# Left-over casts moved behind the last w_out transfer, their stagings moved to a batch's last step, batch 2's middle part reordered in the other half of hbuf

**Chip, cores, metric.** One core of one Trainium2 chip. The metric is the device time of one execution in microseconds (us), lower is better. Times are medians of repeated runs. A profile is one execution; its span, from the first to the last instruction, is about 2 us under the timed figure of the same run.

## The reference

Attention with a "softmax plus one" denominator, then an MLP with exact GELU. Shapes: batch 8, 12 heads, 448 positions, 64 columns per head; d_model 768, d_ff 2048; inputs and output are float32.

```python
scores = scale * q @ k.T ; m = max(scores)
e = exp(scores - m)
attn = e / (sum(e) + exp(-m) + 1e-9)
x = (attn @ v), heads joined          # 3584 x 768
out = gelu(x @ w_in) @ w_out
```

## The kernel before

The kernel works in steps. Step s computes scores and exponentials of one pair of heads; a batch has six pairs (NPAIR = 6). TensorE fills the time in which ScalarE makes exponentials with the MLP of the batch before: in the steps r = 0 and 1 of a batch with layer 1, in the later ones with halves of layer 2 ("l2"). For batch 0 all six steps r = 0 to 5 hold layer 2. Scores run two steps ahead, so step b = 0, r = 4 computes the scores of batch 2's first pair.

448 positions are three full blocks of 128 and 64 left-over rows. Left-over rows of k and v are staged in float32 on SyncE's queue and cast to float16 by GpSimd. All other loads from here on are issued by GpSimd, in program order.

```python
stage_pool = ... bufs=2          # two staging buffers in turn
h_pool     = ... bufs=1          # hbuf0, hbuf1: layer 1's results before GELU

def stage_left(src, b, gate=False):
    st = stage_pool.tile([P, NPAIR, D], FP32, name="stage")
    ...                          # four transfers on SyncE's queue
        nc.sync.dma_start(out=dst, in_=view[i, e])

def cast_left(src, b):
    if src is v:
        nc.gpsimd.tensor_copy(out=vl[b % 2], in_=st)         # one cast
        return
    for x in range(2):                                       # two casts
        nc.gpsimd.tensor_copy(out=blocks[...], in_=st[r]...)
```

Batch 2 comes in three parts (pairs 0 to 2, pair 3, pairs 4 and 5), since its loads arrive while batch 0 still works. VectorE reorders each part into hbuf, which is free at that time, and SyncE's queue transposes it from there:

```python
PARTS = (0, 3, 4, NPAIR)
def order_by_pairs(b, w, c0, c1):
    if w == 0:
        spare = h_pool.tile([P, NBURST * S], FP16, name="hbuf1")
    ...
        nc.vector.tensor_copy(out=dst[:, :, :, e, :], in_=src[:, c0:c1, e])

def fetch_part(b, i):            # i = 0 after batch 0's GELU, 1 in r = 4, 2 in r = 5
    for w in range(2):           # q, then k
        order_by_pairs(b, w, c0, c1)
        transpose_on_dma(b, w, c0, c1)
```

Order of the loads before these steps, and what each step fetches:

```python
load_part(0); load_w_out(0, 0..1)        # first half of w_out's columns
stage_left(v, 1); stage_left(k, 2)
load_v(1, 0, 8); load_w_out(1, 0..3)     # second half, in quarters of d_ff
load_part(1); load_v(1, 8, H); load_part(2)
cast_left(v, 1); cast_left(k, 2)

def fetch(b, r):                         # after step r of batch b
    r0 = 0 if b else 2
    if r == r0 and b + 2 < B:
        stage_left(v, b + 2)
        load_v(b + 2)
    if r == r0 + 1 and b + 2 < B:
        cast_left(v, b + 2)
    ...
    elif b and r in (0, 1) and b + 2 < B:
        transpose_on_dma(b + 2, r)       # r = 0: q; r = 1: k and its left-overs
    if r == 3 and b + 3 < B:
        load_pairs(q ..., b + 3); load_pairs(k ..., b + 3)
        stage_left(k, b + 3)
    if r == 4 and b + 3 < B:
        cast_left(k, b + 3)
```

The softmax here doesn't subtract the row's maximum and nothing guards it: scores larger than these inputs give would overflow.

## Time and profile before

| | |
|---|---|
| median before the prediction | 420.46 us (419.53 to 420.59) |
| the run that was profiled | 421.8 us, span 420.0 us |
| waits of TensorE of 1 us or more after the start | 2.00 us at 66.3, 5.34 us at 89.8 |
| stretch at half clock (granted clock 0.50), begun in the second | 88.3 to 95.2 us |

The lines themselves stand in the prediction. In the slices each digit is the busy share of a fortieth of the span in tenths. A line of the timeline gives start, busy time, engine, source line, operation, what it writes and reads, and in brackets the idle time of the engine before it and what ended that.

### The profile page before, as it was taken

To read this page: it belongs to the slowest core of one execution; us is meant where nothing else is said; L and a number is where in the kernel's file an instruction comes from. 1 tells how busy PE (TensorE), PEld (TensorE's weight loads), DVE (VectorE), ACT (ScalarE), POOL (GpSimd) and SP (SyncE) were. 2 spreads that over 40 slices of the span, in tenths; PEclk is the share of its full clock that TensorE was granted. 3 is DMA by queue.
4 is the path that set the end of the run, shared out by engine and by line. 5 is a ranking of instruction groups with operands and counts; after the bars stand their busy time and mean duration, and the time that the engine had idled before them with its cause. 6 is when DMAs were issued, how large, how long until landed. Compare 5 with 4: busy or idle time off the path is not lost.

```text
span 420.0 us, 11017 instructions
## 1 busy us (share of the span) xinstructions
PE 400.3 (95%) x4679; PEld 247.0 (59%) x4679; DVE 202.5 (48%) x485; ACT 299.5 (71%) x450; POOL 101.2 (24%) x140
## 2 busy tenths in 40 slices
PE   8888998949999999999999999999999999999995
PEld 3444864525566565666566565666766665665663
DVE  4886335539057732477057731477057741540021
ACT  5998887937888776898588676898589576734300
POOL 8751213095431091024601073020000000000000
PEclk9999999979999999999999999999999999999999
DMA  9999999999992899229962899129211100110032
GB/s 154 152 197 199 197 181 178 190 138 166 153 139 77 119 169 111 61 70 181 133 69 62 118 156 138 59 68 170 58 39 39 40 22 18 54 44 20 2 81 70
DMA packets 137312, 45.08 MB, mean 107 GB/s; under 512 B 118384, under 2 KB 137264, under 8 KB 137264
## 3 DMA queue, kind: packets, MB, share of 16 engines
q0 software_dynamic: 81200, 21.11, 54.7%
q1 hardware_dynamic: 55280, 22.66, 29.5%
q8 instruction: 36, 0.59, 0.6%
q10 hardware_dynamic: 784, 0.62, 0.5%
q14 instruction: 12, 0.10, 0.1%
HBM read 45.61 MB, written 11.01 MB: 135 GB/s over the span
## 4 chain that ended last, share of the span: by engine, by line
PE 78%; DMA 15%; POOL 3%; issue 1%; SPq 1%; DVE 1%; POOLq 0%
PE bank L260 62%; DMA vn<-in_v_dram 9%; PE st L358 6%; PE bank L407 5%; DMA w_in_sb<-in_moe_w_in_dram 3%; DMA tqk<-klraw 2%; PE st L429 2%; PE st L260 2%; DMA stage<-in_v_dram 1%; PE bank L422 1%; POOL rawq L98 1%; POOL rawk L98 1%; DMA out_dram<-osb 1%; SPq L305 1%; PE st L407 1%
## 5 line engine op out<-in xcount | busy, mean ns | idle before, releaser
L346 ACT ACTIVATE et<-st,expb 128x896 f16<-128x896 f32 x144 | 134.4, 1002 | 27.8 <-PE st L358 27.6
L260 PE MATMUL bank<-xt,w_in_sb 128*64 128x448 f16 x1536 | 152.8, 355 | 0.0
L260 PEld LDWEIGHTS <-w_in_sb 128*64 128x64 f16 x1536 | 94.8, 110 | 53.7 <-issue 4.6
L260 PE MATMUL bank<-w_out_sb,gt_odd 128*64 128x384 f16 x1024 | 88.0, 326 | 0.0
L512 DVE COPY osb<-bank 128x384 f32<-128x384 f32 x56 | 31.2, 557 | 99.7 <-PE bank L260 97.7
L260 PEld LDWEIGHTS <-gt_odd 128*64 128x64 f16 x1024 | 57.9, 110 | 27.5 <-issue 2.1
L260 PE MATMUL bank<-w_out_sb,gt_even 128*64 128x384 f16 x768 | 68.5, 327 | 0.0
L445 DVE TENSOR_TENSOR xt<-bank,rec 128x448 f16<-128x448 f32 x44 | 27.5, 625 | 79.4 <-PE bank L422 66.2
L260 PEld LDWEIGHTS <-gt_even 128*64 128x64 f16 x768 | 43.3, 110 | 22.2 <-issue 3.3
L358 PE MATMUL st<-tqk 64*64 64x448 f16 x576 | 43.2, 369 | 1.5 <-ACT et L346 0.4
L469 ACT ACTIVATE gt_odd<-bank 128x448 f16<-128x448 f32 (+1 forms) x74 | 29.1, 394 | 21.5 <-PE bank L260 20.6
L346 ACT ACTIVATE el<-st,expb 128x448 f16<-128x448 f32 x48 | 30.7, 639 | 14.3 <-PE st L429 13.7
L392 DVE TENSOR_TENSOR ksum<-ksum,el 64x448 f16<-64x448 f16 x96 | 37.9, 395 | 2.1
L474 DVE COPY hbuf<-bank 128x448 f32<-128x448 f32 x54 | 33.5, 620 | 10.6 <-PE bank L260 10.0
L392 DVE TENSOR_TENSOR ksum<-t,et 128x448 f16<-128x448 f16 x96 | 35.1, 400 | 0.9 <-ACT et L346 0.6
L392 DVE TENSOR_TENSOR t<-et 128x448 f16<-128x448 f16 x96 | 33.3, 388 | 1.1 <-ACT et L346 0.6
L407 PE MATMUL bank<-et,vn 128*64 128x448 f16 x264 | 33.5, 361 | 0.2 <-DVE tqk L280 0.2
L469 ACT ACTIVATE gt_even<-bank 128x384 f16<-128x384 f32 x34 | 16.7, 490 | 21.5 <-PE bank L260 21.5
L114 POOL DMA_DIRECT2D rawq<-in_q_dram x40 | 30.5, 772 | 3.2 <-DMA vn<-in_v_dram 2.9
L436 ACT ACTIVATE rec<-st,oneb 128x448 f32<-128x448 f32 x42 | 26.7, 639 | 4.9 <-PE st L429 4.9
L358 PEld LDWEIGHTS <-tqk 64*64 64x64 f16 x576 | 15.6, 107 | 22.8 <-issue 18.0
L439 ACT ACTIVATE rec<-rec 128x448 f32<-128x448 f32 x48 | 27.6, 577 | 1.5
(62 smaller groups left out, 247.7 us busy)
## 6 DMA issues: line engine op xcount, KB each, us to landing
vn<-in_v_dram POOLq DMA_DIRECT2D x6, 576.0 KB, 8.7
rawq<-in_q_dram POOLq DMA_DIRECT2D x40, 84.0 KB, 7.5
rawk<-in_k_dram POOLq DMA_DIRECT2D x33, 96.0 KB, 7.0
w_in_sb<-in_moe_w_in_dram POOLq DMA_DIRECT2D x4, 768.0 KB, 16.0
out_dram<-osb SPq DMA_DIRECT2D x16, 168.0 KB, 2.2
out_dram<-osb SPq DMA_DIRECT2D x16, 144.0 KB, 2.0
out_dram<-osb SPq DMA_DIRECT2D x16, 120.0 KB, 2.0
w_out_sb<-in_moe_w_out_dram POOLq DMA_DIRECT2D x2, 768.0 KB, 28.0
```

The costliest lines, as they stand in the source:

```text
L114: nc.gpsimd.dma_start(out=dst[:, :, j, e, :], in_=view[j, e])
L260: nc.tensor.matmul(out[x], lhs[:, x], rhs, start=start, stop=stop)
L346: nc.scalar.activation(out=out, in_=in_, func=AF.Exp, bias=expb, scale=scale)
L358: nc.tensor.matmul(st[cols, e, 0:S], kt[r, j, cols], qt[r], start=True, stop=True)
L392: nc.vector.tensor_tensor(out=dst, in0=a, in1=x, op=ALU.add)
L407: nc.tensor.matmul(po_t[g][e * D:(e + 1) * D, 0:S], v_t[b][:, 2 * c + e, j, :], et[:, 2 * j + e], start=(first and j == 0), stop=(not firs ...
L436: nc.scalar.activation(out=rec_t[g], in_=den_t.pop(g)[:, 0:S], func=AF.Ln, bias=oneb, scale=1.0)
L439: nc.scalar.activation(out=rec_t[g], in_=rec_t[g], func=AF.Exp, scale=-1.0)
L445: nc.vector.tensor_tensor(out=xt_t[b][:, c, :], in0=po_t.pop(g)[:, 0:S], in1=rec_t.pop(g), op=ALU.mult)
L469: nc.scalar.activation(out=dst[:, 0, :], in_=ph[:, c0:c1], func=AF.Gelu)
L474: nc.vector.tensor_copy(out=h_t[b, i][:, n, :], in_=ph[:, 0:S])
L512: nc.vector.tensor_copy(out=osb, in_=po[:, 0:NHW])
```

## The change

The intent is threefold: batch 1's cast of v ready before TensorE asks for it; SyncE's queue clear ahead of the middle part's transposes; and the last part's reordering free of the middle part's transposes.

```diff
-    def order_by_pairs(b, w, c0, c1):
+    def order_by_pairs(b, w, c0, c1, buf):
...
-            spare = h_pool.tile([P, NBURST * S], FP16, name="hbuf1")
+            spare = h_pool.tile([P, NBURST * S], FP16, name=f"hbuf{buf}")
...
         load_w_out(1, i, 4)
+    cast_left(v, 1)
+    cast_left(k, 2)
     load_part(1)
     load_v(1, 8, H)
     load_part(2)
-    cast_left(v, 1)
-    cast_left(k, 2)
...
-            order_by_pairs(b, w, c0, c1)
+            order_by_pairs(b, w, c0, c1, 1 - i % 2)
...
-        r0 = 0 if b else 2
-        if r == r0 and b + 2 < B:
+        if r == 0 and b and b + 2 < B:
+            cast_left(k, b + 2)
+            if b == 1:
+                cast_left(v, b + 1)
             stage_left(v, b + 2)
+        if r == (0 if b else 2) and b + 2 < B:
             load_v(b + 2)
-        if r == r0 + 1 and b + 2 < B:
+        if r == 1 and b and b + 2 < B:
             cast_left(v, b + 2)
...
+        if r == NPAIR - 1 and b + 3 < B:
             stage_left(k, b + 3)
-        if r == 4 and b + 3 < B:
-            cast_left(k, b + 3)
+            if b == 0:
+                stage_left(v, b + 2)
```

## The prediction

> **What bounds the kernel now.** I read the page first, then the matmul timeline, because the page says that TensorE is busy 400.3 of 420.0 us. What is left to win is the idle 20 us and any time at a reduced clock. The page's slices show where that is: the first slices, and one stretch near 84 to 100 us where PE drops to 4 tenths and the granted clock to 7.
>
> ```profile
> PE 400.3 (95%) x4679; PEld 247.0 (59%) x4679; DVE 202.5 (48%) x485; ACT 299.5 (71%) x450; POOL 101.2 (24%) x140
> PE   8888998949999999999999999999999999999995
> PEclk9999999979999999999999999999999999999999
> DMA  9999999999992899229962899129211100110032
> ```
>
> The DMA row is full until some 126 us, so data that is wanted early is a possible bound of its own. From 100 us to the end the timeline shows no idle time of PE. Only two waits of 2 us and more lie before that, both in batch 0's layer-2 steps (steps r = 0 to 5, about 54 to 84 us), and both at the product with the left-over rows of v (L422):
>
> ```profile
> 66.30 0.38 PE L422 MATMUL bank<-el,vl 64*64 64x448 f16 x4 [2.00 <-POOL vl L149]
> 89.84 0.58 PE L422 MATMUL bank<-el,vl 64*64 64x448 f16 x2 [5.34 <-DVE osb L512]
> ```
>
> The first waits for GpSimd's cast of batch 1's left-over v. The GpSimd timeline tells why that cast is late: in program order it stands behind the loads of batch 2's parts, and these are held up until older transfers have landed.
>
> ```profile
> 46.53 0.74 POOL L180 DMA_DIRECT2D w_out_sb<-in_moe_w_out_dram  x1 [1.78 <-DMA rawq<-in_q_dram]
> ...
> 64.99 0.74 POOL L98 DMA_DIRECT2D rawk<-in_k_dram  x1 [3.35 <-DMA w_out_sb<-in_moe_w_out_dram]
> 65.73 0.52 POOL L149 CAST vl<-stage 128x384 f16<-128x384 f32 x1
> 66.18 1.07 POOL L154 CAST klraw<-stage 64x384 f16<-64x384 f32 x2
> 67.39 1.02 POOL L98 DMA_DIRECT2D vn<-in_v_dram  x1
> 83.63 0.50 POOL L149 CAST vl<-stage 128x384 f16<-128x384 f32 x1 [15.22 <-DMA stage<-in_k_dram]
> ```
>
> The second is put down to VectorE's copy of an output half (L512), which frees the PSUM bank. VectorE itself stood still: its copies of batch 2's last part into hbuf (L298) waited until the transposes of the middle part had read the same buffer. SyncE's queue issued those late:
>
> ```profile
> 87.41 0.73 DVE L298 COPY hbuf<-rawq 112x512 f16<-112x512 f16 x2 [5.72 <-DMA tqk<-hbuf]
> 88.06 0.41 DVE L298 COPY hbuf<-rawk 128x384 f16<-128x384 f16 x2
> 88.39 0.80 DVE L392 TENSOR_TENSOR ksum<-ksum,el 64x448 f16<-64x448 f16 x2
> 89.22 0.56 DVE L512 COPY osb<-bank 128x384 f32<-128x384 f32 x1
> ```
>
> ```profile
> 72.22 5.79 SPq L143 DMA_DIRECT2D stage<-in_v_dram  x4
> 78.11 1.01 SPq L488 DMA_DIRECT2D out_dram<-osb  x2
> 79.16 3.01 SPq L143 DMA_DIRECT2D stage<-in_k_dram  x4
> 82.40 2.51 SPq L305 DMA_TRANSPOSE tqk<-hbuf  x2
> ```
>
> The middle part was copied by 77.98 us, but its transposes were issued at 82.40: eight staging transfers stood ahead of them in one in-order queue, and some of those waited for earlier landings (the chain of waits has DMA tqk<-klraw, then SPq L143, then DMA stage<-in_v_dram, then SPq L305). So the chain is: casts late, batch 2's left-over transpose late (67.28), stagings late, middle transposes late, VectorE held, bank held, PE idle.
>
> Last, the busy time and clock by stretch:
>
> ```profile
> 84.50:89.80 5.30, 0.00 (x0) 0.00 (x0) 2.31 (x7) 0.88 (x1) 5.30 (x8) 0.86 1.69 124
> 89.80:95.20 5.40, 5.36 (x34) 2.39 (x35) 2.34 (x5) 1.90 (x2) 5.40 (x7) 0.50 2.18 153
> 74.35:83.26 8.91, 8.91 (x118) 5.35 (x113) 6.09 (x20) 8.75 (x14) 0.00 (x0) 1.00 1.07 196
> ```
>
> Columns: stretch, length, busy time of PE, PEld, DVE, ACT, POOL, then PE clock, DMA share, GB/s. The long wait is followed by 5.4 us at half clock.
>
> **What the Trainium skill says.** "TensorE: Matmul & The Clock Gate", section "Part 1: The HAM clock gate", has the clock at half after an idle window of about 3.4 us and full again after about 3.4 us of sustained work. The trace agrees in kind: 0.50 after 5.34 us idle, nothing after 2.00 us; the half-rate stretch lasted 5.4 us here. "DMA: Bandwidth & Descriptors", section "SWDGE vs HWDGE vs iDMA", says that transfers of GpSimd and of SyncE sit in different queues of the same 16 engines, served in turn, so moving one kind earlier makes the other slower. The trace agrees: the four stagings at 34.8 us took a median of 9.1 us to land, those late in the run some 2 us. "GPSIMD Engine Reference", section "4.1 Engine selection", calls one-input elementwise work there roughly line-rate; here 384 columns take 0.52 us, so the casts cost little; only their place matters.
>
> **The change, part by part.** It adds and removes no work: the same casts, stagings and copies, at other places.
>
> 1. *Casts behind the last w_out issue.* That issue ends at 46.53 + 0.74 = 47.27. The staged v and k were issued at 31.95 to 36.72 and land after medians of 7.7 and 9.1 us, so by about 46. The three casts (0.52 + 1.07 = 1.6 us) run at 47.3 to 48.9 and end 17 us ahead of their use. They push the rawq load from 48.06 to 48.9; the next load waits for a landing at 51.9 anyway, so nothing follows. The 2.00 us wait goes. By stretches: 63.26:74.35 takes 11.09 us, the next two steps of the same work 8.91, so **2.2 us**.
> 2. *Middle part in the other half.* Its readers until then, the GELUs of batch 0 from hbuf, end at 50.0 us. The last part's copies then need only the first part's transposes, which landed by 54.46 + 15.8 = 70.3. The 5.72 us wait of VectorE goes.
> 3. *Staging of v2 and k3 in the last step, their casts at r = 0 of the next batch.* SyncE's queue before the middle transposes keeps only output stores, so they go out at about 75.5 (the copies at 77.31, less the 2 us won) instead of 82.40. GpSimd is not held 15.22 us by the cast and issues batch 3's 14 loads from about 73 on instead of 84.
>
> What parts 2 and 3 are worth together: 83.3:113.4 takes 30.1 us; the same passage one batch later (136.4:163.5) takes 27.1 and contains 64 layer-2 matmuls (5.2 us) that batch 1 lacks, so 21.9 without a wait. **8.2 us** = 5.34 idle + 5.4 × (1 − 0.50) = 2.7 of slow clock + 0.2. Sum of both: 10.4 us, all on PE's path: 420.46 − 10.4 = 410.1.
>
> **Rivals: what could take it back.**
>
> - *hbuf0 becomes the wait.* Batch 1's first layer-1 result goes into hbuf0, which the middle transposes now read. I put its need at 84.7 (94.7, less 2.2, 5.3 and half of the 4.9 us at half clock before it); issued at 75.5 and 76.6 with 4 to 9 us to land, they are done by 81 to 86. PE has a second bank, 1.2 us of grace. Against it: at most a few tenths; if the landing takes 13 us, as the first part's did, 2 to 3 us.
> - *Batch 3's transposes become the wait.* Before, they are issued at 96.55, 102.12 and 110.63 and land after 13.6, 14.7 and 9.1 us: k at 116.8, left-overs at 119.7. PE reads them at 125.57 and 128.34, a slack of 8.8 and 8.6 us, less than the 10.4 that PE would gain. If they land at the same times, the gain stops at 8.6 (411.9). And their chain has lengthened: middle transposes, stores, staging k3 (about 84 to 87), cast k3 (about 93), staging v3, transpose of q (about 96). In favour: the DMA engines moved only 124 GB/s in 81.5:91 while GpSimd stood in the cast, against 214 just before and 171 after; filling 9.5 us at some 60 GB/s more takes 0.6 MB, about 3 us, out of the later queue, so I expect k by about 114 against a need of 115.2. Loss 0 to 2 us; I take 0.4.
> - *ScalarE becomes the bound* in 57 to 84 us: busy 8.75 of 8.91 us per two steps. Behind the first wait it lay idle 1.56 and 0.64 us, 2.2 in all, just what PE gains; so no loss beyond a tenth or two.
> - *The waits are hidden anyway or another stands right behind*, say the bank held at L422 by a late load of the last part (k lands at 64.99 + 15.2 = 80.2; VectorE comes to it at about 80). This would leave a short idle, but only over 3 us of it brings the half clock back; 0.2.
>
> **Range and chances.** 410.1 + 0.4 + 0.2 = **410.7 us**. If batch 3 or hbuf0 bind fully the time is 412 to 414; everything clean with a little more won is 409.2. Range 409.2 to 414. Two per cent is 412.05, only 1.3 us above my number, so: faster 0.70, same 0.29, slower 0.01.
>
> **What would show each step.** Casts at about 47 to 49 us with no wait of PE on vl; middle transposes at about 75 to 77 us; no wait of the hbuf copies on tqk<-hbuf; the granted clock at 1.00 throughout 80 to 100 us; batch 3's loads from about 73 us. The prediction is wrong if PE waits anew at about 85 (hbuf L474 behind tqk<-hbuf), or at about 115 to 118 us (scores of batch 3 behind tqk<-rawk or tqk<-klraw), or if a wait over 3 us brings a second stretch at half clock.

## The result

The four runs of the changed kernel took 414.11, 414.33, 421.84 and 424.69 us: median 418.08, against 420.02 of the kernel before in four runs. The ratio of the fast runs, the two of 414 us, is 0.9861, 95% interval 0.9834 to 0.9889; with all four runs the means are 418.74 and 420.04 us, ratio 0.997. If the long runs are the kernel's own, as e1 below supports, the ratio of the fast runs flatters the change. Ratios here are the mean time of one kernel's fast runs over that of the other's of the same rounds, so not quite the ratio of the quoted medians; a run counts as slow when it is over 1.5% above the fastest of its kernel. The profiled run took 414.33 us, span 412.1.

The page of the changed kernel, in the slices of before:

```profile
PE 397.5 (96%) x4679; PEld 248.7 (60%) x4679; DVE 200.8 (49%) x485; ACT 299.4 (73%) x450; POOL 102.3 (25%) x140
PE   7788999999989999999999999999999999999995
PEclk9999999999999999999999999999999999999999
DMA  9999999999997899229991699229611010110032
```

The hole near 84 us and its dip of the clock are gone, and the DMA row is as full as before. GpSimd's timeline and SyncE's queue show the parts of the change where the prediction put them:

```profile
45.99 0.74 POOL L180 DMA_DIRECT2D w_out_sb<-in_moe_w_out_dram  x1 [2.16 <-DMA rawq<-in_q_dram]
46.73 0.52 POOL L149 CAST vl<-stage 128x384 f16<-128x384 f32 x1
47.18 1.08 POOL L154 CAST klraw<-stage 64x384 f16<-64x384 f32 x2
...
73.80 3.85 POOL L114 DMA_DIRECT2D rawq<-in_q_dram  x5 [7.37 <-PE bank L422]
```

```profile
75.78 2.54 SPq L305 DMA_TRANSPOSE tqk<-hbuf  x2
...
99.70 3.38 SPq L305 DMA_TRANSPOSE tqk<-rawq  x1
103.31 7.75 SPq L305 DMA_TRANSPOSE tqk<-rawk  x1
```

Casts at 46.7, middle transposes at 75.8, batch 3's loads from 73.8. But TensorE's timeline has three new waits:

```profile
92.98 11.54 PE L260 MATMUL bank<-xt,w_in_sb 128*64 128x448 f16 x120 [0.92 <-DVE hbuf L474]
...
117.24 0.38 PE L358 MATMUL st<-tqk 64*64 64x448 f16 x4 [0.65 <-DMA tqk<-rawk]
...
120.78 0.38 PE L260 MATMUL st<-tqk 128*64 128x448 f16 x2 [0.60 <-DMA tqk<-klraw]
```

The first is layer 1 of batch 1 held by VectorE, which waits to overwrite hbuf1 until the last part's transposes have read it (10.7 us from issue to landing). The other two are batch 3's scores behind its transposes. In spans: 420.0 less the 10.4 of the two old waits, plus 0.92 + 0.65 + 0.60 and 0.3 of later start, is 412.1, what the trace has. The trace is thus accounted for, within 0.1 us; what it leaves open is why the timed gain of the fast runs is only 5.8 us, and what the runs of 421.8 and 424.7 us are. For the experiments, theory A says that both come from transfers whose landing times vary from run to run and which TensorE now catches up with; theory B, that something outside the kernel makes the long runs.

### The profile page after: what moved, and what is told of

Read it like the earlier page. It is cut to its first block, busy times and chain, and to the rows that moved or that the text cites. A ratio compares the mean times of both kernels' runs of the same rounds, so it can differ in the third digit from the quotient of the medians.

```text
span 412.1 us, 11014 instructions
## 1 busy us (share of the span) xinstructions
PE 397.5 (96%) x4679; PEld 248.7 (60%) x4679; DVE 200.8 (49%) x485; ACT 299.4 (73%) x450; POOL 102.3 (25%) x140
## 4 chain that ended last, share of the span: by engine, by line
PE 82%; ACT 7%; DMA 6%; SPq 2%; DVE 2%; issue 1%; DVEq 0%
PE bank L260 66%; PE st L358 6%; PE bank L407 5%; ACT et L346 4%; DMA tqk<-hbuf 3%; DMA tqk<-klraw 2%; SPq L305 2%; PE st L429 2%; PE st L260 2%; DMA hbuf<-in_k_dram 1%; PE bank L422 1%; ACT el L346 1%; ACT rec L439 1%; PE st L407 1%; DVE ksum L392 1%
## 5 line engine op out<-in xcount | busy, mean ns | idle before, releaser
L260 PEld LDWEIGHTS <-w_in_sb 128*64 128x64 f16 x1536 | 96.9, 110 | 51.6 <-issue 4.4
L358 PE MATMUL st<-tqk 64*64 64x448 f16 x576 | 42.3, 363 | 2.3 <-DMA tqk<-rawk 0.6
L392 DVE TENSOR_TENSOR ksum<-t,et 128x448 f16<-128x448 f16 x96 | 34.1, 391 | 0.9 <-ACT et L346 0.6
L154 POOL CAST klraw<-stage 64x384 f16<-64x384 f32 x12 | 7.3, 611 | 90.2 <-DMA stage<-in_k_dram 88.7
L114 POOL DMA_DIRECT2D rawk<-in_k_dram x30 | 24.6, 823 | 20.2 <-DMA rawq<-in_q_dram 18.9
```

The lines of the kernel that those rows point to most:

```text
L114: nc.gpsimd.dma_start(out=dst[:, :, j, e, :], in_=view[j, e])
L260: nc.tensor.matmul(out[x], lhs[:, x], rhs, start=start, stop=stop)
L358: nc.tensor.matmul(st[cols, e, 0:S], kt[r, j, cols], qt[r], start=True, stop=True)
L392: nc.vector.tensor_tensor(out=dst, in0=a, in1=x, op=ALU.add)
```

## The experiments

Each set shared a chip and the runs of the kernel before. The sets e1 to e4, e5 to e8, e9 to e12 and e13 to e16 had medians of before of 422.45, 421.19, 421.79 and 421.73 us.

| run | what it is | runs, us | ratio to before (95%) |
|---|---|---|---|
| e1 | the change again | 415.01 to 421.55 | 0.9868 (0.9825 to 0.9911) |
| e2 | before again | 419.21 to 423.01 | 0.9962 (0.9918 to 1.0006) |
| e3 | change, transposes first | 411.44 to 417.72 | 0.9779 (0.9734 to 0.9825) |
| e4 | change, own buffers | 412.46 to 424.54 | 0.9785 (0.9730 to 0.9840) |
| e5 | casts alone | 420.80 to 423.65 | 1.0022 (0.9984 to 1.0060) |
| e6 | other half alone | 415.78 to 419.78 | 0.9899 (0.9857 to 0.9941) |
| e7 | casts and half | 415.52 to 416.87 | 0.9871 (0.9844 to 0.9898) |
| e8 | change, both mendings | 411.03 to 415.34 | 0.9809 (0.9770 to 0.9847) |
| e9 | change, casts in other order | 413.71 to 417.70 | 0.9843 (0.9806 to 0.9881) |
| e10 | casts and own buffers | 414.48 to 419.28 | 0.9875 (0.9833 to 0.9917) |
| e11 | e8, no wait on w_out (wrong result) | 410.71 to 412.37 | 0.9749 (0.9719 to 0.9779) |
| e12 | change without the half | 418.76 to 423.23 | 0.9946 (0.9900 to 0.9992) |
| e13 | change, batch 4's loads held | 411.56 to 418.34 | 0.9795 (0.9750 to 0.9841) |
| e14 | e3, batch 4's loads early | 412.88 to 415.25 | 0.9832 (0.9784 to 0.9880) |
| e15 | change, no wait on w_out (wrong result) | 414.16 to 420.19 | 0.9869 (0.9821 to 0.9918) |
| e16 | e8, v of batch 1 split | 411.05 to 413.10 | 0.9768 (0.9735 to 0.9802) |

All but e11 and e15 gave a correct result.

### e1: the change again

No edit.

> The changed kernel unaltered, to see how often it falls into the longer time (421.8 and 424.7 us against 414.1 and 414.3). Theory A: the longer times are the kernel's own: one of the new waits (last part's transposes behind hbuf at about 92 us, batch 3's transposes at about 117 us) grows past 3 us when the transfers are a little slower, and brings a stretch at half clock; then the clock of those runs is 0.985 to 0.990 and a fresh trace shows the same waits with other lengths. Theory B: something outside the kernel; then the kernel before, run beside it, shows such runs as often. Expected: most runs 413.5 to 415.5, some 420 to 425.

Six runs took 418.91, 418.50, 415.01, 416.85, 421.55 and 415.17 us, so three of six are over 418. The eleven runs of before beside them lie between 420.25 and 425.06. Theory B was to be told by before showing as many long runs; it spreads as much, but it has waits of its own, so its spread alone decides nothing. The fresh trace does better. It is of the first of the six, 418.91 us:

```profile
74.10 0.84 PE L260 MATMUL bank<-w_out_sb,gt_even 128*64 128x384 f16 x8 [2.63 <-DMA w_out_sb<-in_moe_w_out_dram]
...
121.28 0.59 PE L358 MATMUL st<-tqk 64*64 64x448 f16 x4 [2.90 <-DMA tqk<-rawk]
```

The busy time by stretch, behind the second of these (columns as in the prediction; the third figure from the end is the granted clock):

```profile
121.30:124.50 3.20, 3.20 (x26) 1.42 (x28) 0.76 (x2) 2.58 (x3) 2.46 (x3) 0.50 1.82 208
```

A wait that the first trace does not have stands at 74.1: the last quarter of w_out's second half. It landed at 74.1 here; in the first trace a median of 24.2 us after its issue at 45.99, so at 70.2, just before TensorE's use at about 71.8 (the second 16 matmuls of that half begin at 71.14 and come to the last quarter midway). And the wait for batch 3's k grew from 0.65 to 2.90 us, with 3.4 us at half clock behind it. Waits and clock are 2.63 + 0.38 (hbuf) + 2.90 + 1.7 = 7.6 us, against 2.2 in the first trace: 5.4 more, and the time is 4.6 more. This supports theory A: the same kernel, the same order, other landing times.

### e2: the kernel before again

No edit.

> The kernel before unaltered, for a second trace. The first trace is of a run of 421.8 us, while its timed runs took 419.5 to 420.6. If my sum was too large because that trace was of a longer run, the second wait of this trace (5.34 us, with 5.4 us at half clock) is shorter here, by 1 to 2 us in all with the slow clock, and the time is about 420. If it is as long as in the first trace, the missing 2 us lie elsewhere.

The profiled run took 419.21 us. Its waits and the stretch behind the first:

```profile
66.43 0.38 PE L422 MATMUL bank<-el,vl 64*64 64x448 f16 x4 [1.98 <-POOL vl L149]
89.56 0.38 PE L422 MATMUL bank<-el,vl 64*64 64x448 f16 x2 [3.25 <-DVE osb L512]
```

```profile
67.50:70.90 3.40, 3.40 (x26) 1.83 (x22) 2.60 (x7) 1.46 (x2) 1.02 (x1) 0.50 1.47 188
```

The second wait is 2.1 us shorter than in the first trace, and the stretch at half clock is 3.4 us, this time behind the short wait. The sum is 1.98 + 3.25 + 3.4 × 0.5 = 6.9 us, where the same terms of the first trace give 2.00 + 5.34 + 2.7 = 10.0 (10.4 when taken by stretches). So the trace that the prediction rested on shows a longer run than most of the timed ones: 421.8 us against a median of 420.

### e3: transposes ahead of the staging

On the changed kernel:

```diff
         if r == 0 and b and b + 2 < B:
             cast_left(k, b + 2)
             ...
-            stage_left(v, b + 2)
         ...
-        if r == 1 and b and b + 2 < B:
-            cast_left(v, b + 2)
         ...
             transpose_on_dma(b + 2, r)
+            if r == 1:
+                stage_left(v, b + 2)
+        if r == 2 and b and b + 2 < B:
+            cast_left(v, b + 2)
```

> The changed kernel, with the next batch's transposes issued ahead of the staging of left-over v (staging after the transposes of r = 1, its cast at r = 2). If the waits at about 117 and 121 us come from the place of batch 3's transposes in SyncE's queue (behind a staging that waits for a cast), they go: transposes at about 95.5, 100.5 and 106 us in place of 99.7, 103.3 and 111.1, and 1.4 + 0.6 = about 1.5 to 2 us are won: 412.0 to 412.8. Rival: the DMA engines are full there anyway and the transposes land no earlier; then 414.

The ratio is 0.9779. The profiled run, 411.44 us, has no wait of TensorE over 0.3 us between 60 and 126 us. The transposes of q, k and left-overs were issued at 93.7, 98.1 and 101.3 us, and that of k landed 10.1 us after issue, at 108. The waits went, as theory A asks. That this came of the place in SyncE's queue is not shown, since the cast of v at r = 2 also put off the loads of batch 4 behind it, from 102 to 111 us; e13 and e14 come back to this. Two of the six runs still took 417.7; they count as slow, so the ratio is of the other four.

### e4: own buffers for the middle and last parts

On the changed kernel:

```diff
-            spare = h_pool.tile([P, NBURST * S], FP16, name=f"hbuf{buf}")
             n = 2 * (c1 - c0)
+            spare = (h_pool.tile([P, NBURST * S], FP16, name=f"hbuf{buf}") if c0 == 0
+                     else h_pool.tile([P, n * (NJ + NK) * D], FP16, name=f"part{buf}"))
```

> The changed kernel, with a buffer of its own for each of batch 2's middle and last parts, so that layer 1's results wait for no transpose. Theory: the wait of 0.92 us at about 92 us (hbuf behind tqk<-hbuf) goes. If the later waits on batch 3's transposes are set by the transfers' absolute times, they grow by as much, and the time stays at 414 (within 0.3); if they are set by the pace of TensorE, 0.9 us are won: 413.2.

The trace, of a run of 413.40 us, has no wait on hbuf, but its wait for batch 3's k is 1.37 us where the first trace of the change had 0.65: most of the 0.92 came back one station later. Three runs took 412.46 to 414.29, the other three 421.15 to 424.54; the ratio rests on the three fast ones and says little. The mending of this wait alone doesn't touch the long runs.

### e5, e6, e7, e12: the parts of the change by themselves

The three parts are the casts (C), the other half (H) and the move of the stagings (S). Their edits are those pieces of the diff above: e5 is C, e6 is H, e7 is C and H, e12 is C and S.

> The kernel before, with the two casts moved alone. My reading: the 2.0 us wait on the cast of v goes (2.2 us), but the middle part's transposes stay behind the eight stagings and come out at about 81 us, so VectorE's copies of the last part still wait for hbuf until about 86, while TensorE comes to the bank at about 82: 4 to 5 us of wait stay. 418 to 420. Rival: the casts are the head of the whole chain, and with them early the second wait goes too: 411 to 413.

The ratio is 1.0022: the casts alone win nothing. The wait on vl is gone from the trace, and the second has grown to 7.06 us, with 10.2 us at half clock:

```profile
88.93 0.58 PE L422 MATMUL bank<-el,vl 64*64 64x448 f16 x2 [7.06 <-DVE osb L512]
```

TensorE comes to the bank 2.6 us earlier (81.9 against 84.5), but is let on only 0.9 us earlier (88.9 against 89.8). The transposes of the middle part were issued at 80.5, as my reading had it, and the rival falls. The time, 420.80 to 423.65, is over the 418 to 420 expected, by the longer wait and its slow clock.

> The kernel before, with the middle part in the other half of hbuf alone. My reading: the second wait (3.3 to 5.3 us and the slow clock behind it) goes, the 2.0 us wait on the cast stays, and batch 3's transposes keep their early place with some 8 us to spare, so nothing new appears: 6 to 8 us less than before, 413 to 415 with before at 421. Rival: the new buffer alone does nothing while the stagings stand ahead of the transposes: 420.

The ratio is 0.9899, 4.3 us: most of what the whole change brings, of one name in one line. But less than the 6 to 8 us expected, and with two waits that I had not put there:

```profile
87.11 2.46 PE L260 MATMUL bank<-xt,w_in_sb 128*64 128x448 f16 x24 [1.11 <-DVE hbuf L474]
96.04 11.54 PE L260 MATMUL bank<-xt,w_in_sb 128*64 128x448 f16 x120 [3.01 <-DVE hbuf L474]
```

With the middle transposes still behind the stagings (81.2 us), both halves are read later than layer 1 wants to write them. In this trace the 2.0 us wait on the cast of v was absent, since the w_out transfer that held GpSimd's queue had landed earlier (61.3 us against 64.7); so that wait too comes and goes with the transfers.

> The change without the move of the stagings and of their casts. If the move of the stagings is what made batch 3's transposes late (issued at 99.7 us in the changed kernel against 96.5 before), they come at about 95 here, no wait at 117 to 121 us appears, and the time is 1 to 2 us under the changed kernel's (about 412 to 413), less up to 1.5 us for hbuf behind the last part's transposes at 91 us. If the move is what frees TensorE at 84 us, the long wait comes back and the time is over 418.

The ratio is 0.9871, the same as the whole change's 0.9868 and 0.9861. As expected, there is no wait for batch 3 in the trace, but 1.55 and 0.78 us on hbuf and 0.92 on w_out. The time expected, 412 to 413 or up to 1.5 us more by hbuf, was missed: the six runs took 415.52 to 416.87. The move of the stagings thus exchanged the wait on hbuf for that on batch 3's transposes and won nothing that these runs show. The comparison has one flaw. In the traces of e7, e9 and e16 the first product of layer 2 comes at 56.5 to 56.8 us, in the other fifteen at 54.8 to 55.8; in e7 TensorE waited 1.69 us for a load of k and ran at half clock from 28.2 to 31.7 us. The program up to there is that of the change, so the start varies from run to run too, by about 1 us here.

> The changed kernel, with the middle part in hbuf1 again: casts and stagings moved, one buffer. The last part's copies then wait for the middle part's transposes, which here land at about 85 us in place of 87, while TensorE comes to the bank at 82: some 4 to 5 us of wait with half clock behind it, 418 to 422. If it is near the changed kernel's 414 to 418, the other half is not needed once the stagings are moved.

The ratio is 0.9946, as expected: the trace has 4.77 us of wait at the bank, behind one of 2.64 us on w_out. The other half is needed with the stagings moved as well.

### e8, e10, e11, e15: what is left when the new waits are mended

e8 joins e3 and e4. e10 is e7 with the own buffers of e4.

> The changed kernel with the transposes ahead of the staging of left-over v, and with own buffers for the middle and last parts. If the waits at 92 us and at 117 to 121 us are the whole of what the change lost, none is left but one on the last w_out transfer (about 70 us) in runs where transfers are slow: 409.5 us of span at best, 411 to 415 timed, at or under the kernel with the transposes ahead alone (411.4 to 417.7), and fewer runs over 418 than the changed kernel has.

The ratio is 0.9809 and all six runs lie between 411.03 and 415.34. The trace, of the longest of them, has one wait left:

```profile
74.07 1.16 PE L260 MATMUL bank<-w_out_sb,gt_even 128*64 128x384 f16 x8 [2.59 <-DMA w_out_sb<-in_moe_w_out_dram]
```

> The kernel before, with the casts moved and own buffers for the middle and last parts; the stagings stay where they were. If the waits on hbuf (1.55 and 0.78 us with the two halves) are all that is left behind TensorE but for the last w_out transfer, they go: 416.2 less about 2.3, so 413.5 to 414.5, as good as the changed kernel with both mendings (414.2). Then the move of the stagings has no worth of its own. If that move has, this is over 416.

The ratio is 0.9875 with a median of 416.51, over the 414.5 expected, and over the 416 that the text on record took as the sign that the move of the stagings has a worth. The trace has no wait on hbuf or on batch 3, but 0.83, 0.50 and 2.04 us on w_out's and v's transfers. Whether the moved stagings help once the other waits are mended is not settled by this: e8 and e10 differ in the transposes' place as well.

> Wrong on purpose: the kernel with both mendings, where batch 0's second output half multiplies with the first half's columns of w_out, which have landed long before, so that no product waits for the last w_out transfers; all transfers are issued as before. If the wait on the last w_out transfer (2.6 us and 3.4 us at half clock in that kernel's trace) is the last one and makes its spread (411.0 to 415.3), the time is 410.5 to 412 in all runs. Rival: the spread comes from the start (the first 30 us) and stays.

```diff
-                        po[:, 0:NHW], gt[:, fc, g0:g0 + P], w_out_sb[:, fc, n0:n0 + NHW],
+                        po[:, 0:NHW], gt[:, fc, g0:g0 + P],
+                        w_out_sb[:, fc, 0:NHW] if b == 0 else w_out_sb[:, fc, n0:n0 + NHW],
```

All six runs of e8 with this edit took 410.71 to 412.37, ratio 0.9749, with all transfers still issued. So the wait on the last w_out transfer is most of what is left of the spread in e8 (4.3 us there, 1.7 here), and about 411 us is what this program takes when TensorE waits for no transfer after the start. What remains has the size of what the start varies by (e7); that it comes from there is not shown. The prediction's 410.7 was the time of such a kernel.

> Wrong on purpose: the changed kernel, where batch 0's second output half reads the first half's columns of w_out. If the wait on the last w_out transfer, in the runs where it lands at 74 us in place of 70, is what makes the runs of 418 to 425 us, all runs are 413 to 415.5. If the long runs come from the waits on hbuf and on batch 3's transposes, they stay, as often as in the changed kernel (5 of 10 over 418).

The same edit on the unmended change: 414.16 to 420.19, one of six over 418, ratio 0.9869. Freeing w_out alone doesn't win, for the trace shows 0.61 us on hbuf and 1.37 us on batch 3's k. This trace also has 3.4 us at half clock from 8.0 us, in the start. One long run of six, against five of ten of the change, is too few to tell whether w_out makes part of them; that it isn't the only cause is shown by the one that remains. How large the share of each wait is in the runs of 421.8 and 424.7 us is open, since no trace was taken of these.

### e9: batch 3's transposes made later

```diff
-            cast_left(k, b + 2)
             if b == 1:
                 cast_left(v, b + 1)
+            cast_left(k, b + 2)
```

> The changed kernel, with batch 2's cast of v ahead of batch 3's cast of k. The cast of v waits for a staging that lands at about 99 us, so the cast of k, the next staging and batch 3's transposes come about 4 us later (q at about 103.5 in place of 99.7). If the runs over 418 us of the changed kernel come from the wait for batch 3's transposes growing past some 3 us and the half clock that follows, nearly all runs are now of this kind: the trace shows 4 to 6 us of wait at 117 to 121 us and 3 to 7 us at half clock, and the time is 419 to 425. Rival: the long runs come from elsewhere; then the time is 415 to 418 with a share of long runs as before.

This expectation failed. The transposes were issued at 103.0 and 109.8 us, q by 3.3 and k by 6.4 us later than in the changed kernel, but k landed in 7.5 us in place of 13.9, at the same 117.2. TensorE's waits were 0.45 and 0.95 us, and all runs took 413.71 to 417.70. A later place in the queue did not make the landing later. What else had moved: GpSimd's next cast of v came at 109.5, and with it batch 4's loads, from 101.9 to 110.0 us. And batch 3's own v, one transfer of 576 KB on GpSimd's queue, had landed by 109.2, before k was issued; in the changed kernel it was under way until 110.8.

### e13, e14: place or competition

e13 holds batch 4's loads by the one-element write that batch 3's already have. e14 is e3 with the cast of v at r = 4, so that these loads don't wait for it.

```diff
-        if b == 3:
+        if b in (3, 4):
             nc.vector.memset(tiles[b][:, 0, 0, 0:1], 0.0)
```

> The changed kernel, with batch 4's loads held (by a write that VectorE makes at the end of step r = 3) until about 115 us; they began at 102 us. The place of batch 3's transposes in SyncE's queue stays. If these are late because batch 4's loads compete for the DMA engines, the transpose of k, issued at about 103, lands at 110 to 113 in place of 117.2, and no wait of TensorE is left at 117 to 121 us. If they are late by their place in the queue alone, they land at 116 to 117 as before and the waits stay.

> The kernel with batch 3's transposes ahead of the staging of v, but with batch 4's loads again from about 100 us on (the cast of v behind them, at r = 4). The counterpart of the gated loads: if the competition sets the landing, the transpose of k is issued early (about 98 to 101) and still lands at 113 to 117, near or behind TensorE's need at 115.9; if the place sets it, it lands at about 108 to 111 as in the kernel with transposes first.

Time from issue to landing of batch 3's transpose of k, with what GpSimd had under way beside it. In the changed kernel (issued at 103.3), batch 3's v and batch 4's loads:

```profile
tqk<-rawk SPq DMA_TRANSPOSE x1, 13.9
```

In e14 (issued at 102.3), both again, v until 110.0 and batch 4's loads from 101.7:

```profile
tqk<-rawk SPq DMA_TRANSPOSE x1, 13.7
```

In e3 (issued at 98.1), v alone, from 98.6 to 108.8; batch 4's loads begin at 111.4:

```profile
tqk<-rawk SPq DMA_TRANSPOSE x1, 10.1
```

In e9 (issued at 109.8), batch 4's loads alone, from 110.0:

```profile
tqk<-rawk SPq DMA_TRANSPOSE x1, 7.5
```

In e13 (issued at 111.0), neither: v had landed by 110.3, and the next loads were held until 122.7:

```profile
tqk<-rawk SPq DMA_TRANSPOSE x1, 5.3
```

So the landing goes with what runs beside the transpose and not with its place: 13.7 to 13.9 us with both, 10.1 with v, 7.5 with batch 4's loads, 5.3 with neither. The left-overs go the same way, 9.6 us in the changed kernel and 2.8 in e13. Each is one trace. The texts on record speak of batch 4's loads alone; by these figures batch 3's own v costs the transpose more than they do (4.8 against 2.2 us, though in e3 four stagings ran beside it too). And e13's trace doesn't isolate the held loads, since k was issued there only after v had landed.

In e14 k landed at 116.0, and TensorE waited 0.63 us on the left-overs. e13's trace has no wait for batch 3. Its expectation that k lands at 110 to 113 missed, as the profiled run is a slow one (418.34 us) in which everything came later: k was issued at 111.0 and landed at 116.3. The fast runs are compared alone: 411.56 to 416.19, ratio 0.9795 (0.9750 to 0.9841) against 0.9868 (0.9825 to 0.9911) of e1 in another set, for one added condition. The intervals touch, and no trace of a fast run of e13 was taken. The slow one is one of the long runs with a trace at last, and it shows the same wait as e1:

```profile
75.74 1.49 PE L260 MATMUL bank<-w_out_sb,gt_even 128*64 128x384 f16 x8 [3.00 <-DMA w_out_sb<-in_moe_w_out_dram]
```

with 6.8 us at half clock from 74.9 on, so 3.0 idle and some 3 more by the clock: about its 6 us over most of the fast runs. I read it as the slow end of what the fast runs show, not as a difference between kernels.

### e16: transfers in the order of their use

On e8:

```diff
-    load_v(1, 0, 8)
-    for i in range(4):
+    load_v(1, 0, 4)
+    for i in range(3):
         load_w_out(1, i, 4)
+    load_v(1, 4, 6)
+    load_w_out(1, 3, 4)
+    load_v(1, 6, 8)
```

> The kernel with both mendings, with batch 1's v in three transfers: heads 0 to 3, then three quarters of w_out's second half, heads 4 and 5, the last quarter, heads 6 and 7, in the order in which TensorE asks for them. If the order of the queue sets the wait on the last w_out transfer, this transfer lands about 0.8 us later than heads 4 and 5 but ahead of heads 6 and 7, some 1 us earlier than before, and the time is 412 to 413.5 (414.2 with both mendings alone). If transfers are limited by the sum alone, the wait moves to the v of pairs 2 and 3 and nothing is won.

The ratio is 0.9768 and all six runs lie between 411.05 and 413.10 us, median 411.48, where e11, with no wait on w_out by construction, had 411.08. The last quarter of w_out landed at 70.6 in a run whose transfers were otherwise late (its first half landed at 56.3, in the changed kernel's first trace at 54.8). This trace has no wait of TensorE on a transfer over 0.3 us between 38 and 200 us. Against e8 (0.9809, 0.9770 to 0.9847, in another set) the gain is likely and not shown, since the intervals overlap. This version beats both kernels: before by 2.3%, and the change (0.9868 in its six runs, against another set of runs of before) by about 1%.

## Why the prediction was wrong

410.7 us was predicted, 414.2 measured in the two fast runs and 418.08 as the median of all four.

- **"Casts behind the last w_out issue": 2.2 us.** The mechanism was right: they ran at 46.7 to 48.3 us (47.3 to 48.9 predicted) and no product waits for them. The gain is not separate: alone it is nothing (e5), because the next wait takes it.
- **"Middle part in the other half": right,** and the part that carries the gain (e6, e12). VectorE's last copies ran at 79.7 us without a wait.
- **"Staging of v2 and k3 in the last step":** right in both times named there (75.8 for the transposes, 73.8 for the loads), but these runs show no gain of it (e7 against e1; e10 against e8 leaves open whether it has one once the other waits are mended). It was credited with what the other half had already won.
- **The sum, "420.46 − 10.4 = 410.1", is the first step that failed.** It takes the waits of a run of 421.8 us from the median of other runs. A second trace of the same kernel has 6.9 us of them (e2). Taken from 421.8, the run that they were read in, the same sum gives 411.4: 1.3 us of the miss.
- **The terms for new waits, 0.4 + 0.2, are the second.** Both rivals came about, batch 3's at the place named, hbuf's at 92 and not at 85 us: batch 3's transposes cost 0.65 + 0.60 us in the first trace and 2.90 us with 1.7 by the clock in the second; hbuf cost 0.92 and 0.38 us, and it was hbuf1 behind the last part and not hbuf0. Together 2.2 us at best in place of 0.6, so 1.6 more. With the 1.3 us above and the 0.3 of later start this is 3.2 of the 3.5 us that the fast runs miss.
- **Not named at all: w_out.** Moving TensorE 2 us forward at 66 us puts its use of the last quarter, about 73.7 before (the matmuls of 73.05), at about 71.8, while the transfer lands at 70.2 to 75.7 from run to run. Without that wait and the other two it is 411.1 us (e11).
- **The argument that 0.6 MB of spare transfer time would let batch 3's k land at about 114 failed.** It landed at 117.2. The chain before it was slower than put (k's cast at 95.7 for about 93, q's transpose at 99.7 for about 96), and k then took 13.9 us beside batch 3's v and batch 4's loads, 10.1 beside v alone and 5.3 beside neither (e3, e13); I had counted how much was to be moved, not what would stand beside it. Nor did the prediction's range allow for a spread that grows: it took one landing time for each transfer.
- **Three readings were off.** The stretch at half clock lasted 6.8 us, from 88.3; the 5.4 us are the part in which TensorE worked, so the term of 2.7 us stands. "Only over 3 us of it brings the half clock back" is false: 1.98 us did in e2. And the stagings from 126 us on took medians of 2.3 to 3.7 us to land, not "some 2".
- **ScalarE as the bound: right that it isn't.** The stretch of the first wait now takes 8.9 us, as its neighbour does.

## What to carry to other kernels

Where data arrive just ahead of their use, taking a wait away moves the compute engine forward to the next landing; list the landing of every transfer against the new time of its use, not only of those that the change touches. Take two or more traces of the kernel before, set the losses against the time of the run that was traced, and ask how the landing times vary. And look at what is issued behind a transfer that is wanted: holding loads that nobody needs yet (e13) and asking for the parts in the order of their use (e16) look to have won more than the move of the stagings, though the intervals of both touch those of the kernels they start from.

## What the Trainium skill lacked or had wrong

- "TensorE: Matmul & The Clock Gate", section "Part 1: The HAM clock gate", gives the half clock after an idle window of about 3.4 us. It adds that frequent short idles bring it too, without a length. Here waits of 1.98, 2.59 and 2.64 us were followed by 3.4 us at half clock (e2, e8, e12), while 3.25 us (e2), 3.01 (e6) and 2.63 (e1) were not. The same section has the window run freely, with 3.41 us. Counting such windows back and forward from the starts of the stretches at half clock (an estimate), TensorE was busy for 42, 24 and 39% of the window just before them in e2, e8 and e12. Windows that were busy for 42% (e6), 46% (e1) and 51 and 53% (e2, where the wait of 3.25 us fell into two) had none behind them. In the start, where TensorE makes short transposes, windows busy 45 to 63% were followed by half clock as well (e7, e9, e15, e16), so the busy share is not the whole rule. A wait under 3.4 us is not safe. Stretches at half clock were multiples of the window: 3.4, 6.8 and, begun in 7.06 us idle, 10.2 us (e5).
- "DMA: Bandwidth & Descriptors", section "SWDGE vs HWDGE vs iDMA", says that both kinds share the engines in turn, but not what this costs the one that waits; that one kind slows the other was the prediction's inference. Here the transpose of one batch's k took 13.9 and 13.7 us to land beside GpSimd's v and next loads, 10.1 beside v (e3), 7.5 beside the next loads (e9) and 5.3 beside neither (e13).
- None of the pages that I read says that landings of the same transfer in the same kernel vary by several us from run to run; the last w_out transfer landed between 70.2 and 75.7 us in the changed kernel and e13, with the same order up to there.
